# Writing y in natural channel order with 32-column matmul blocks, and loading w_in unpermuted

## The chip, the cores and the metric

The kernel runs on one core of a Trainium2 chip. The time is device microseconds of that core. Before the change the median of three runs is 618.56 us (617.26 to 618.66). The page and the trace come from one further, profiled execution, which took 619.2 us.

## What is computed

Two stages, in fp32 accuracy. First a gated linear attention over 4 batches, 8 heads, 768 tokens and head dimension 48, in which a 48x48 state decays by alpha and takes up the outer product of k and v. Then a feed-forward layer over the 3072 tokens, 384 channels (8 heads x 48) to 2048 and back, with a rational function between.

```python
for t in range(S):                                   # attention, per batch and head
    state = alpha[t][:, None] * state + outer(k[t], v[t])
    y[t] = q[t] @ state
x = y in token order, head by head                   # 3072 x 384
h = x @ w_in                                         # 384 -> 2048
P = a[0] + a[1]*h + a[2]*h**2 + a[3]*h**3
Q = 1 + abs(b[0])*abs(h) + abs(b[1])*h**2
out = (P / (Q + 1e-6)) @ w_out                       # 2048 -> 384
```

## The kernel before, in words

**Attention.** Tokens go in chunks of C = 128, two chunks to a segment (12 segments, `m`). A *piece* `i` is one chunk and four of the eight heads: chunk `g = i // 2`, head group `gq = i % 2`; 48 pieces in all. Within a piece heads are addressed by `a` (0 or 1) and `j` (0 or 1): head `2*gq + a + 4*j`. The group `j` sits on partitions 64j to 64j+47, since a head takes DP = 64 partitions of which D = 48 are used and GAP = 16 are not. alpha, k and q come to this channel-on-partition form in two ways: the first two segments are loaded by token (`load_nat`, L359) and transposed by TensorE (`turn_nat`, L367), the others are loaded in 32-row blocks (`load_akq`, L334) and transposed by VectorE (L383 to L389). v is loaded by token (`load_v`, L379) into a buffer with 64 columns a head, the last 16 zero.

Each piece runs these steps: `sc_mm` (L450) the scores, `sc_evac` on ScalarE (ACT) and `sc_mask` on GpSimd (POOL), `decay` (L473, POOL) which scales the state into `st_d`, and then `attn_mm` on TensorE (PE). `attn_mm` has three groups of matmuls: the state products (L486, not in the first chunk of a batch) and the value products (L493) add up y in PSUM bank 3, and the state update (L501, not in the last chunk of a batch) goes to a score bank. Each group is four products per piece, one for each (a, j); the stationary operand has 64 columns, so j = 0 writes partitions 0 to 63 and j = 1 writes 64 to 127. `kv_add` on VectorE (DVE) folds the update into the state. Scores are in banks 4 and 5; of the first EARLY = 4 pieces the odd ones are in banks 6 and 7, which are later the accumulators of the MLP output.

**From y to x.** y has four column slots of 128 tokens, one for each head pair, and in each the 16 partitions behind every group of 48 are zero. `x_hi` (L526, ACT) and `x_lo` (L531, DVE) copy the 512 columns of the bank into a high and a low part. `x_gap` (L541) then moves the rows of the fourth slot into the gaps of the first three by six transfers a segment (two j, three slots), so that three slots of 128 full partitions remain for the MLP. The channels are thereby permuted, and `load_w` (L221, L224) loads each unit of w_in in four transfers with the same permutation.

**MLP.** The hidden dimension goes in 8 units of 256. Per segment and unit (96 in all), `mlp_in` (L563) makes 18 matmuls of 256 columns (three partial products of high and low parts), fourteen elementwise steps on ACT, POOL and DVE (L570 to L613) make the rational function, and `mlp_out_hi` and `mlp_out_lo` (L624, L634) add the output in banks 6 and 7. The weights arrive as 64-bit words and are turned into a high and a low part on ACT, DVE and POOL (L237 to L268), once, in the first part of the run. At the end a guard over alpha (L660, L664) decides whether a general path is needed.

**Order.** Every step is registered with its engine, an assumed cost and the steps it comes after (`add`). The order in which all steps are issued is a written list, `ORDER`, a packed permutation of the step numbers, computed beforehand from those costs. Each engine and the transfer queue of SP (SyncE) run their share of this list in order. All loads and transfers of the fast path are issued by SP.

Of the kernel before, what the change touches and what calls it, by code (L numbers as in the profile page):

```python
# [12 lines left out]
F32 = mybir.dt.float32  # L13
F32R = mybir.dt.float32r
# [8 lines left out]
class Plan:  # L23
# [35 lines left out]
    'n3}92XwXMhM14qI2h_(^B<<mhdIyoUz)7`-qUZn~!d{B1Nn1FfPN`3zbs<ptE~EpaZ$n{74|gCJ6oCxz9&$r;T^v3@',
    '44oZ5LLP{v%fTZk3V9*6z6a$YAEeZA^#iB?adayE1*$><eOkrSpCO^Xq|U0;`U%9>_aUu*4ChsMs0bnYf+_*gbR}SX',  # L60
    '3KvyOoklyX42kq*m0pMHw-BcHQ3pt;Gw9s94op#rbsk+8GU^Ce5|ZdlI+@m(ROi*DAi2(`TS5w55Ay5MP*4}pnYCac',
    '9S-WlcPOlj=x6X18bDF)@j1ML7f?+9fc^9aitC1OfU@Wk`X?CBP*%5slDZm{(^++O$fo0Ad7WK<gNnKaG}IMzTs)^L',
    '>6%bkH_}tpFSw!lL1+CNYC#iSMK{(-u#0Z4tLiW;1C1duzJ#tihi<BK>IB#Xs_9(1g>I%x>FPQ@me#MKhHj|?ETe1c',
    '?z$-$9I9*SR=Tzhhr@Jh-9vZNaj=cPs)p-kkPt`eE9#nxh@*5{-5h%A>DuCT)lT=)Gjs_4f!;b1_R%+0dmV~>^<NmF',
    'TR=ZOQ-{aVdbS>;5$ouV@DKXyx_YbztfvR)aeAe04fXYSt+0V!r6*{@Hqb$@)*bagy;gV9ZDE$attRSwsvXSHbM<aL',
    'N#9a;)I7aMPu5Xzz8<6_V=la_*66`{fqtUa>&!Sr@73*Lp`N0%;UYa%FV_2YR-C5S=?%IE<iPWKiS7wmaHGDUd%-51',
    '6PM|Wx;NZc*>SU8s{6ne{ZLI)ePN&8s+a2r>asqlSLki}kbbEisfRi#9?*|;BrJ}P)nWZu@6hS-Aa#PB`iMS6+jS;<',
    'qL1pQDgz$VSM(+QOdZ$HbTN#IyYvZN0-vi>`l^nG8S%7!p`zn8{X-YUlR6n**U9mxzM)HFY<#M3>gW25E`z`HE&WQJ',
    ')hVzf{?UhNx{874bUEw{<?#r`!rS^Nb%DU#(Yf)i?h4_|3mx8cgWvk4j$r=jQus=PiHY}gf2e?Y@V<Vn%i;idt={Or',
    'x)HwBZ`1=l5b9zilM>%)H1+VUN`;~3y&eR$QJFA9=7Sy#bx@mkDzT}LL%^7%CNE|-4KSi%(*#rFNBv1R#waGT`K&+t',  # L70
    's3wc~=F{RA9nE~xUv)){Zp3`o)?_s?OjC3wrb&a|Br%;ZmdS29V{((sd{D7X3eyoks<<YOd9UJ`l%^pTHJ?;A(*;wR',
    'A1bGbZ@&9xm=05$VkU=4V?L_{rnpIK5}K0cs|qnQR63In6PfDf7=2U6DZR;HzNlO#qxq*wm>TB0%56%UOeR0pG-XUF',
    'lgIp21u(BEf@MuUQwV>nawfm2ZGNeirhqAL>X<*Of+=La_=={WDQqfZCDY1O!oRAP>4im1Yg5_OHGQy(X>014s-`!#',
    'F$J-=sc(8>d(+M|Fnvr{>|hEbP(#z#bjOaSkujvGlWA;bs{W=2b~e?_3F=}7m~J@MG%+WMsH<sanwnFD)Xg+E&9Q~)',
    'XS$mf_`~-w1C6Gh=BpoMdYLLX*o;M{A!ZEL!l5RhaptEVW~$;JUkz*Ea5LYG#tEi6jxY<%NE~k_n~`Rs8G+l(6tl>T',
    '!%1e8X^D%?XtTsj#AT)?jxkfsax)1Rn(bzq>5EIvc${v8c9<Dvg_(es9L+RyF*2<*o=%uqW<IVmyUc7e$E-G^aIRTn',
    'cAK4M9-cI7%^tG=Z<$kOo!M*7nBh3jw8GP7z1e5N(K&P0>^J941UgN#R0lj@TH^)N4iB0QCL)EWjpmTKXd=;Vv&EdD',
    'O=hc!NteuF^Tup8cg$sT#2htk@SeG1j+wjWzBz8Lng`~Wk3!eXL-WW)qqg|iTsP6_iD{2F%y0kH+%!??ua7|xJTq_2',
    '0DNx#nfK;}d1pSEm*#`{Y+jjx_|NylkLI-*guwlAA;zaKW->0r$UF=c55})%DMn%BZ)Pa2K;rKv7DeSBM)MYo&W6Ky',
    'w)$z9WAJ7?ONrU?Ir?RO8{zYmg#Q@FLogcuHJ$@b#&IYnhvVd&h2v5zUW8dWHpS-fJO$(M5{$s{C@v@Eh`b%+adr-)',  # L80
    'NSuOqU`|dzDLEJK#Q2<wLue}Q!UUX+OLJ;YNC|llCZaSP!fAOQmf=v!!Ra^!?Zrf#o6~bBm*w4<hcj?SUWs{m8)o8Z',
    'SdKIE8O+BOxh|LI>39lfVI{_(9-qeiT!Cj`0ZvROu|5~%IarxzVtX#cbJTLYKt;GPSK*7a6&rF<uF4I#7&qc-ycnx<',
# [24 lines left out]
    '0#{Fcm5xfegf5b+uR`2dis;Biagkjj_f)idCdM^X-z2IFbKiwsG?&<or=cpkn?OG#hRfn&I_oA<Ea#lKaTMEm*Fnvo',
# [27 lines left out]
GB = 3  # L135
# [844 lines left out]
```

## Time and profile before

| | |
|---|---|
| median of 3 runs | 618.56 us (617.26 to 618.66) |
| profiled execution | 619.2 us, span of the trace 617.3 us |
| busy: PE / DVE / ACT / POOL | 553.9 / 507.6 / 477.8 / 387.4 us |
| mean granted TensorE clock | 0.957 |
| L486 state products, L493 value products, L501 state update | 320, 384, 320 matmuls; 28.1, 32.2, 16.5 us |
| L526 `x_hi`, L531 `x_lo` | 24 each; 14.1 and 16.4 us |
| L541 `x_gap` | 72 transfers of 32 KB, median 2.0 us from issue to landing |
| L221, L224 w_in | 16 transfers of 288 KB and 16 of 96 KB, median 5.7 and 5.6 us |

A row of a group gives the source line, engine, operation, operands, shape and count, then busy time and the mean length of one in ns, then the idle time just before and what ended it. Busy time of overlapping matmuls is counted once, so busy time over count can be less than the mean length. PEld is the loading of the stationary operand. The ends of matmuls are modelled in the trace; their starts are recorded. A row of the timeline gives start, length to the end of the last, and the count of instructions that were merged.

### The profile page before, as it was taken

The page shows a single profiled execution, that of the slowest core. Times are in us where ns is not written, and L with a number is a line of the kernel's source. Part 1 is how long each engine was busy: PE and PEld are TensorE (multiplying, and loading weights), DVE is VectorE, ACT ScalarE, POOL GpSimd, SP SyncE. Part 2 cuts the span into 40 slices and gives each one's busy share as a digit, 9 for nine tenths or more (in the row PEclk, how much of TensorE's full clock was granted, in tenths as well). Part 3 has the DMA queues.
Part 4 walks back from the last instruction along what each step waited for, and adds up shares of the span by engine and source line. Part 5 has one row for each costly group of instructions (what it writes and reads, how often), then busy time and mean ns, then how long its engine had stood idle before and what let it go on. Part 6 is the DMA issues. An engine that isn't in the chain of part 4 may idle for free.

```text
span 617.3 us, 12165 instructions
## 1 busy us (share of the span) xinstructions
PE 553.9 (90%) x4338; PEld 515.4 (83%) x4338; DVE 507.6 (82%) x782; ACT 477.8 (77%) x803; POOL 387.4 (63%) x419
## 2 busy tenths in 40 slices
PE   3866857899699999999999999999899999999993
PEld 2656746788599989999999999899899999999983
DVE  3588898999989988889888987989789787777872
ACT  3467666777668788987889898999878787888971
POOL 4645234676687686867768676667648667655561
PEclk9977887899899999999999999999899999999997
DMA  9999495413452441344324343434321000000000
GB/s 154 227 189 251 77 188 103 54 19 50 61 101 47 93 53 50 54 82 65 64 57 77 57 85 67 90 65 91 55 44 36 14 27 14 14 22 6 27 2 30
DMA packets 182658, 44.14 MB, mean 71 GB/s; under 512 B 170944, under 2 KB 174016, under 8 KB 182592
## 3 DMA queue, kind: packets, MB, share of 16 engines
q1 hardware_dynamic: 182592, 43.30, 38.0%
q8 instruction: 36, 0.59, 0.4%
q14 instruction: 30, 0.25, 0.1%
HBM read 36.18 MB, written 4.72 MB: 66 GB/s over the span
## 4 chain that ended last, share of the span: by engine, by line
PE 49%; DVE 21%; ACT 11%; DMA 9%; SPq 4%; issue 3%; POOL 1%; ACTq 0%; DVEq 0%; POOLq 0%
PE ps L563 20%; PE ps L624 14%; PE ps L634 7%; DMA wi_words<-in_moe_w_in_dram 5%; DVE t L597 4%; DVE ps L600 3%; DVE t L606 3%; PE ps L450 3%; ACT t L573 2%; PE ps L486 2%; DVE t L587 2%; SPq L334 2%; DVE t L583 2%; PE ps L493 2%; DMA tv<-in_v_dram 2%
## 5 line engine op out<-in xcount | busy, mean ns | idle before, releaser
L563 PE MATMUL ps<-x,wi 128*128 128x256 f32 x1728 | 235.9, 289 | 23.5 <-DVE t L606 14.7
L563 PEld LDWEIGHTS ps<-x,wi 128*128 128x128 f32 x1728 | 223.2, 194 | 33.9 <-DVE t L606 20.1
L579 POOL TENSOR_TENSOR qm<-qm,ah 128x512 f32<-128x512 f32 x96 | 128.4, 1338 | 101.8 <-ACT qm L576 100.8
L624 PE MATMUL ps<-wo,gh 128*128 128x384 f32 x768 | 159.8, 348 | 6.3 <-ACT gh L609 3.5
L613 POOL TENSOR_TENSOR gl<-t,gh 128x512 fp32r<-128x512 f32 x88 | 116.5, 1326 | 51.5 <-issue 28.8
L624 PEld LDWEIGHTS ps<-wo,gh 128*128 128x128 f32 x768 | 134.7, 192 | 12.2 <-ACT gh L609 6.7
L583 DVE TENSOR_TENSOR t<-t,ps 128x512 f32<-128x512 f32 x96 | 65.4, 681 | 36.9 <-ACT t L573 29.5
L597 DVE SCALAR_TENSOR_TENSOR t<-t,coef,ps 128x512 f32<-128x512 f32 x96 | 71.3, 742 | 24.4 <-ACT ps L593 24.0
L634 PE MATMUL ps<-wo,gl 128*128 128x384 f32 x384 | 85.9, 346 | 4.1 <-DVE gl L613 4.1
L573 ACT ACTIVATE t<-ps,coef 128x512 f32<-128x512 f32 x96 | 74.3, 774 | 12.0 <-PE ps L563 5.3
L576 ACT ACTIVATE qm<-ah,bab 128x512 f32<-128x512 f32 x96 | 77.8, 810 | 6.8 <-DVE ps L600 5.5
L590 ACT ACTIVATE ps<-qm,one_eps 128x512 f32<-128x512 f32 x96 | 66.0, 688 | 20.0 <-DVE t L587 15.1
L609 ACT ACTIVATE gh<-t 128x512 fp32r<-128x512 f32 x96 | 60.0, 625 | 19.9 <-DVE t L606 18.1
L570 ACT ACTIVATE ah<-ps 128x512 f32<-128x512 f32 x96 | 56.9, 593 | 23.7 <-PE ps L563 23.0
L634 PEld LDWEIGHTS ps<-wo,gl 128*128 128x128 f32 x384 | 68.9, 192 | 5.9 <-DVE gl L613 4.4
L587 DVE SCALAR_TENSOR_TENSOR t<-t,coef,ps 128x512 f32<-128x512 f32 x96 | 71.6, 746 | 2.6
L606 DVE SCALAR_TENSOR_TENSOR t<-ps,t 128x512 f32<-128x512 f32 x96 | 66.0, 687 | 2.2
L600 DVE SCALAR_TENSOR_TENSOR ps<-qm,ps 128x512 f32<-128x512 f32 x96 | 66.0, 688 | 0.0
L593 ACT ACTIVATE ps<-ps 128x512 f32<-128x512 f32 x96 | 56.1, 584 | 1.3
L450 PE MATMUL ps<-tq,tk 48*128 48x192 f32 (+1 forms) x384 | 46.8, 366 | 9.5 <-POOL tq L425 9.5
L459 ACT ACTIVATE sc<-ps 128x768 f32<-128x768 f32 (+1 forms) x48 | 36.9, 769 | 12.7 <-PE ps L450 8.4
L450 PEld LDWEIGHTS ps<-tq,tk 48*128 48x128 f32 x384 | 32.3, 203 | 16.4 <-POOL tq L425 10.8
(93 smaller groups left out, 609.5 us busy)
## 6 DMA issues: line engine op xcount, KB each, us to landing
wo_words<-in_moe_w_out_dram SPq DMA_DIRECT2D x8, 768.0 KB, 8.1
wi_words<-in_moe_w_in_dram SPq DMA_DIRECT2D x16, 288.0 KB, 5.7
tv<-in_v_dram SPq DMA_DIRECT2D x24, 192.0 KB, 3.1
wr<-in_alpha_dram SPq DMA_DIRECT2D x18, 256.0 KB, 2.9
out_dram<-parts SPq DMA_DIRECT2D x24, 192.0 KB, 2.0
raw_a<-in_alpha_dram SPq DMA_DIRECT2D x80, 32.0 KB, 2.1
raw_q<-in_q_dram SPq DMA_DIRECT2D x80, 32.0 KB, 2.1
raw_k<-in_k_dram SPq DMA_DIRECT2D x80, 32.0 KB, 2.1
```

Source lines behind the costliest of these rows:

```text
L450: nc.tensor.matmul(bank(home(i) + j)[:, SW * a : SW * a + w], tk[n % NQ][r, c, :], tq[n % NQ][r, c, 0:w], start=True, stop=True,)
L563: nc.tensor.matmul(h_of(u)[:, ff * SEG : (ff + 1) * SEG], split_w["i", j][:, kt * FU + ff, w, :], x[:, kt, xp, :], start=(kt == 0 and n == ...
L573: nc.scalar.activation(buf(s, "t1", u), h_of(u), AF.Identity, bias=a2, scale=a3)
L576: nc.scalar.activation(buf(s, "qm", u), buf(s, "ah", u), AF.Identity, bias=b0, scale=b1)
L579: nc.gpsimd.tensor_tensor(buf(s, "qm", u), buf(s, "qm", u), buf(s, "ah", u), op=ALU.mult)
L587: nc.vector.scalar_tensor_tensor(t, t, a1, h_of(u), op0=ALU.add, op1=ALU.mult)
L597: nc.vector.scalar_tensor_tensor(t, t, a0, h_of(u), op0=ALU.add, op1=ALU.mult)
L600: nc.vector.scalar_tensor_tensor(h_of(u), buf(s, "qm", u), 1.0 + 1e-6, h_of(u), op0=ALU.add, op1=ALU.mult)
L606: nc.vector.scalar_tensor_tensor(t, h_of(u), 2.0, t, op0=ALU.subtract, op1=ALU.mult)
L613: (nc.vector if GL_DVE[0] <= u < GL_DVE[1] and s is fast_bufs else nc.gpsimd).tensor_tensor(buf(s, "gl", u).rearrange("p a b -> p (a b)"), ...
L624: nc.tensor.matmul(o_of(tt), buf(s, "gh", u)[:, ff, tt * P : (tt + 1) * P], split_w["o", j][:, ff, w, :], start=(j == j0 and ff == 0 and w ...
L634: nc.tensor.matmul(o_of(tt), buf(s, "gl", u)[:, ff, tt * P : (tt + 1) * P], split_w["o", j][:, ff, 0, :], start=False, stop=(j == j1 and f ...
```

## The change

y is written in the order of the 384 channels themselves: three column slots of 128 tokens, all partitions used, no gaps. A head begins at channel 48h, which is a multiple of 32 for even a and 16 behind one for odd a. So the window of 64 columns that holds a head and 16 zero columns (ahead of the head for a = 1, behind it for a = 0) always begins at a multiple of 32. It is written as two matmuls of 32 stationary columns, each to one quarter of the partitions, and the zeros add nothing to the neighbouring head that shares the quarter (`into_y`). The state update is cut into blocks of 32 columns too. The buffers of v and of the decayed state get 16 zero columns ahead of the first head. `x_hi` and `x_lo` copy 384 columns instead of 512, `x_gap` and its 72 transfers are gone, the MLP follows `x_lo` directly, and each unit of w_in is one transfer. EARLY is 8 instead of 4. `ORDER` is a new list; the costs that the list was made with are 0.47 and 0.55 for `x_hi` and `x_lo` and one transfer's cost for a unit of w_in, and those of `attn_mm` are as before. The general path is changed alike and left out here.

```diff
--- before.py
+++ after.py
@@ -51,73 +51,73 @@
 ORDER = [
...
 ]
@@ -126,7 +126,7 @@
 DMA = 0.49
 W_ACT = {}
 PHASES = (0, 6)
-EARLY = 4
+EARLY = 8
 NQ = 3
 LO_DVE = (0, 4)
 GL_DVE = (0, 8)
@@ -195,7 +195,6 @@
-
     NI = FU * P
     w_in32 = w_in.bitcast(U32)
     w_out32 = w_out.bitcast(U32)
@@ -214,17 +213,7 @@
         eng = nc.scalar if j in W_ACT else nc.sync
         if kind == "i":
             t = weights.tile([P, KT, 2 * NI], U32, tag=f"wi{j}", name=f"wi{j}_words")
-            cols = w_in32[:, 2 * j * NI : 2 * (j + 1) * NI]
-            for jj in range(2):
-                h0 = jj * NPAIR * D
-                h3 = h0 + KT * D
-                eng.dma_start(
-                    t[DP * jj : DP * jj + D], cols[h0:h3].rearrange("(a p) n -> p a n", p=D)
-                )
-                eng.dma_start(
-                    t[DP * jj + D : DP * (jj + 1)],
-                    cols[h3 : h3 + D].rearrange("(a p) n -> p a n", p=GAP),
-                )
+            eng.dma_start(t, w_in32[:, 2 * j * NI : 2 * (j + 1) * NI].rearrange("(a p) n -> p a n", p=P))
         else:
             t = weights.tile([P, FU, 2 * DM], U32, tag=f"wo{j}", name=f"wo{j}_words")
             eng.dma_start(t, w_out32[j * NI : (j + 1) * NI, :].rearrange("(a p) n -> p a n", p=P))
@@ -285,11 +274,12 @@
     tk = ring("tk", NQ, [P, NC4, C])
     tq = ring("tq", NQ, [P, NC4, C + DP])
     ones1 = work.tile([P, NC4 * C1], F32, name="ones1")
-    tv = ring("tv", 3, [P, H, DP])
+
+    tv = ring("tv", 3, [P, GAP + H * DP])
     tot = ring("tot", NQ, [P, NC4, 2])
     halves = work.tile([P, 2], F32, name="halves")
     st_s = ring("st_s", 2, [P, 2, D])
-    st_d = ring("st_d", 2, [P, 2, 2, DP])
+    st_d = ring("st_d", 2, [P, GAP + NPAIR * DP])
     scs = ring("sc", NSC, [P, 2, 2, C + DP])
     def set_raw(s, nm):
@@ -314,7 +304,11 @@
             )
     def set_v(s):
-        nc.gpsimd.memset(tv[s][:, :, D:DP], 0.0)
+        nc.gpsimd.memset(tv[s][:, 0 : H * DP].rearrange("p (h w) -> p h w", w=DP)[:, :, 0:GAP], 0.0)
+        nc.gpsimd.memset(tv[s][:, H * DP :], 0.0)
+
+    def heads_of(t):
+        return t[:, GAP:].rearrange("p (h w) -> p h w", w=DP)[:, :, 0:D]
     def set_st():
         nc.gpsimd.memset(halves, 0.0)
@@ -376,7 +370,7 @@
     def load_v(g):
         b, t0 = divmod(g * C, S)
-        nc.sync.dma_start(tv[g % 3][:, :, 0:D], v[b, :, t0 : t0 + C, :].rearrange("h t e -> t h e"))
+        nc.sync.dma_start(heads_of(tv[g % 3]), v[b, :, t0 : t0 + C, :].rearrange("h t e -> t h e"))
     def turn_a(n):
         o = ta[n % 2][:, 1:].rearrange("p (c t) -> p c t", t=C1)[:, :, 0:C]
@@ -471,37 +465,49 @@
         g, gq, m, cc, first, last, n = piece(i)
         f = tot[n % NQ][:, cc::2, :]
         nc.gpsimd.tensor_tensor(
-            st_d[gq][:, :, :, 0:D], st_s[gq].unsqueeze(2).to_broadcast([P, 2, 2, D]),
+            heads_of(st_d[gq]).rearrange("p (a j) e -> p a j e", j=2),
+            st_s[gq].unsqueeze(2).to_broadcast([P, 2, 2, D]),
             f.unsqueeze(3).to_broadcast([P, 2, 2, D]), op=ALU.mult,
         )
+
+
+
     def attn_mm(i):
         g, gq, m, cc, first, last, n = piece(i)
         sc, vt = scs[i % NSC], tv[g % 3]
         y = bank(3)
+        begun = set() if gq == 0 else set(range(4))
+
+        def into_y(lhs, at, rhs, a, j, stop):
+            c0 = D * (2 * gq + a + NPAIR * j) - GAP * a
+            for x in range(2):
+                kt, r = divmod(c0 + 32 * x, P)
+                w0 = GAP + DP * at - GAP * a + 32 * x
+                nc.tensor.matmul(
+                    y[r : r + 32, kt * C : (kt + 1) * C], lhs[:, w0 : w0 + 32], rhs,
+                    start=r // 32 not in begun, stop=stop, skip_group_check=True,
+                )
+                begun.add(r // 32)
+
         if not first:
             for a in range(2):
-                p = 2 * gq + a
                 for j in range(2):
-                    nc.tensor.matmul(
-                        y[DP * j : DP * (j + 1), p * C : (p + 1) * C], st_d[gq][:, a, j, :],
-                        tq[n % NQ][:, 2 * a + cc, 0:C], start=(p == 0), stop=False, skip_group_check=True,
-                    )
+                    into_y(st_d[gq], 2 * a + j, tq[n % NQ][:, 2 * a + cc, 0:C], a, j, False)
         for a in range(2):
-            p = 2 * gq + a
             for j in range(2):
-                nc.tensor.matmul(
-                    y[DP * j : DP * (j + 1), p * C : (p + 1) * C], vt[:, p + NPAIR * j, :],
-                    sc[:, j, a, 0:C], start=(first and p == 0), stop=(p == NPAIR - 1), skip_group_check=True,
-                )
+                into_y(vt, 2 * gq + a + NPAIR * j, sc[:, j, a, 0:C], a, j, gq == 1)
         if not last:
             kv = bank(home(i) + i % 2)[:, KV : KV + 2 * D]
             for a in range(2):
                 for j in range(2):
-                    nc.tensor.matmul(
-                        kv[DP * j : DP * (j + 1), a * D : (a + 1) * D], sc[:, j, a, C:],
-                        vt[:, 2 * gq + a + NPAIR * j, 0:D], start=True, stop=True,
-                    )
+                    h = 2 * gq + a + NPAIR * j
+                    for x in range(2):
+                        r = DP * j + 32 * x
+                        nc.tensor.matmul(
+                            kv[r : r + 32, a * D : (a + 1) * D], sc[:, j, a, C + 32 * x : C + 32 * (x + 1)],
+                            vt[:, GAP + DP * h : GAP + DP * h + D], start=True, stop=True,
+                        )
     def kv_add(i):
         g, gq, m, cc, first, last, n = piece(i)
@@ -518,27 +524,20 @@
 ORDER = [
...
 ]
@@ -729,21 +728,14 @@
...
@@ -796,7 +788,7 @@
     keys = [(kind, j) for j in range(NU) for kind in "io"]
     for n, key in enumerate(keys):
-        add(("w", key), "ACT" if key[1] in W_ACT else "SP", 4 * DMA if key[0] == "i" else DMA, load_w, key, kb=2.4,
+        add(("w", key), "ACT" if key[1] in W_ACT else "SP", DMA, load_w, key, kb=2.1,
             at=W_ACT.get(key[1], 0.0))
         add(("abs", key), "ACT", 0.91, join_abs, (key, n), [("w", key)] + [("lo", x) for i, x in enumerate(keys[:n]) if wr_slot(i) == wr_slot(n)][-1:])
         add(("sign", key), "DVE", 0.55, join_sign, (key,), [("abs", key)], lock=True)
@@ -879,10 +871,8 @@
     last_user = {6: [i for i in range(EARLY) if home(i) == 6]}
     for g in range(NBLK * 2):
         m, cc = divmod(g, 2)
-        add(("xh", g), "ACT", 0.6, x_hi, (g,), [("am", 2 * g + 1), ("last", m - XB)])
-        add(("xl", g), "DVE", 0.7, x_lo, (g,), [("xh", g)])
-        if cc:
-            add(("xg", m), "SP", 6 * 0.63, x_gap, (m,), [("xl", g), ("xl", g - 1)], kb=0.6)
+        add(("xh", g), "ACT", 0.47, x_hi, (g,), [("am", 2 * g + 1), ("last", m - XB)])
+        add(("xl", g), "DVE", 0.55, x_lo, (g,), [("xh", g)])
     ends = {}
@@ -892,7 +882,7 @@
             early = [("cp", *key, 2 * key[0] + x) for key in nat_users[u % 3] for x in range(2)]
             early += [("tn", 1, nm, cc) for nm in "akq" for cc in range(2)]
             add(("in", u, ff), "PE", 1.08, mlp_in, (u, ff, xts[m % XB]),
-                [("xg", m), ("lo", ("i", j)), ("in", u, 0) if ff else ("in", u - 1, FU - 1), ("g", u - 3)]
+                [("xl", 2 * m), ("xl", 2 * m + 1), ("lo", ("i", j)), ("in", u, 0) if ff else ("in", u - 1, FU - 1), ("g", u - 3)]
                 + early, lat=0.13, due=T0 + PACE * u + 1.08 * (ff + 1))
         if j == NU - 1:
             add(("last", m), "PE", 0.0, lambda: None, (), [("in", u, 1)])
```

More of the change, by code (lines that the diff above doesn't have):

```diff
@@ L59 @@
[L59 to L70, printed above, removed]
@@ new lines @@
+    '7hh2_H5p&hTRMjOu!>5qUei0;k15m}I*7&874@D{t3%jbrBsLU1Eo;~)Jcr5j$libMg62xm_Yrak8~Ovsf6kiox#s^',
+    '6#q~Ml~o<b-;_vYQ(q{pnu5FO1d94gd+0n~!ka3mQu-gA#R~}fhDxVUUst5R(k+!<X?+p1tIOC=Wl-f*ke-TH(5T{y',
+    'bwJ%!k@Q{?ZPgvMkG_#tMn6`;`a1=w`zo@w`UkyN<yDAw`kC_jfePpf>Ygg7DyoO7kgB8}sa&eC`k=z}b5%rrRG~Ut',
+    '-&QZwQ&m|-(dY1+imIdOcj}F*ql&5@>WR96arGyaTgB5JqU%>Gy^f*d>+gz{R(VuRok4$933P<ctLm!Hs)S0Y>!~2f',
+    'q)V!d`mM^W>#G1H)>(7|C6HAo(TTK!Z2F5TrIPAoT0=fnS|!&FRb+^zv+EQ(wyvryq||YA4qZkCLqXk2<<tzRbRk_$',
+    'rPh%kjV`RKD+6hD5nV$S)#-Fq{ZiFb)$}h_OXboDpt>%uYwEa=TfbI~RSDf($A_P)n9ieH=n#kvC3Rk%PiKNZs+7Kp',
@@ L121 @@
+    '#}Dvb`~*MHcl8tfAV1Gf@@xEHKi^OGYyA{I#8376{5n6)&-Fw72EX4g@az3TztIo#2mB^K+%NK*{dB+BZ}Bty62H|i',
+    '^)r25zs(==%lu)#-Cyv_{SLpvU-UcuO25k=^sD@3f5fl$SNu`G+h6t9{T_eJU-LKoUVq$Q@+bUFf70Lbr~GYy+TZbK',
+    '{TYAPpY!+pd4JzO@DKeX|I|PB&-@er9}QKs$p',
 ]
@@ L531, in x_lo @@
         nc.vector.tensor_tensor(
-            xts[m % XB][:, :, 1, cs], bank(3).rearrange("p (k t) -> p k t", t=C),
+            xts[m % XB][:, :, 1, cs], bank(3, DM).rearrange("p (k t) -> p k t", t=C),
             xts[m % XB][:, :, 0, cs].bitcast(F32), op=ALU.subtract,
         )
-    def x_gap(m):
-        x = xts[m % XB].bitcast(F32).rearrange("p k w t -> p k (w t)")
-        for j in range(2):
-            for kt in range(KT):
-                r0 = DP * j + GAP * kt
-                nc.sync.dma_start(x[DP * j + D : DP * (j + 1), kt], x[r0 : r0 + GAP, KT])
     N = FU * SEG
@@ L731, in general @@
                 for tt in range(2):
-                    xn = gen.tile([P, KT, 2, DP], F32, name=f"gen_x{tt}")
+                    xn = gen.tile([P, H, D], F32, name=f"gen_x{tt}")
                     tok = bass.ds(r0 + tt * P, P)
-                    for jj in range(2):
-                        h0 = jj * NPAIR
-                        nc.sync.dma_start(
-                            xn[:, :, jj, 0:D], xd[h0 : h0 + KT, tok, :].rearrange("h t e -> t h e")
-                        )
-                        nc.sync.dma_start(
-                            xn[:, :, jj, D:DP],
-                            xd[h0 + KT, tok, :].rearrange("t (k e) -> t k e", e=GAP),
-                        )
+                    nc.sync.dma_start(xn, xd[:, tok, :].rearrange("h t e -> t h e"))
                     xp = bank(3, DM)
@@ L745, in general @@
                         nc.tensor.transpose(
-                            xp[:, kt * P : (kt + 1) * P], xn[:, kt].rearrange("p j e -> p (j e)"), ident
+                            xp[:, kt * P : (kt + 1) * P],
+                            xn.rearrange("p h e -> p (h e)")[:, kt * P : (kt + 1) * P], ident,
                         )
```

117 lines of the change are left out of this document (60 added, 57 removed).

## The prediction

> **What bounds the kernel now.** I read the table of stretches first, for the engine that is full in each stage, then the waits, then the timeline where the edits fall. Columns: stretch; its length; busy time and count of PE, PEld, DVE, ACT and POOL; granted clock; DMA share; GB/s.
>
> ```profile
> 0.00:20.00 20.00, 7.77 (x32) 5.44 (x32) 9.69 (x12) 6.77 (x15) 9.66 (x34) 1.00 1.12 159
> 20.00:40.00 20.00, 15.60 (x132) 12.29 (x128) 11.33 (x18) 11.43 (x23) 11.76 (x17) 0.97 1.08 246
> 40.00:60.00 20.00, 13.17 (x100) 11.71 (x100) 18.06 (x25) 14.35 (x20) 8.44 (x13) 0.67 0.90 193
> 80.00:100.00 20.00, 12.64 (x76) 11.13 (x77) 18.76 (x29) 11.03 (x17) 8.07 (x11) 0.76 0.83 158
> 100.00:150.00 50.00, 44.87 (x338) 41.33 (x338) 46.93 (x70) 38.68 (x61) 31.41 (x27) 0.96 0.35 55
> ...
> 200.00:550.00 350.00, 345.26 (x2880) 326.59 (x2879) 297.37 (x474) 298.46 (x515) 242.24 (x248) 1.00 0.31 56
> ```
>
> Three stages can be seen. Up to 40 us the DMA engines are full (shares 1.12 and 1.08) and no engine is. From 40 to about 150 us VectorE (DVE) is the full one, 18.06 of 20, 18.76 of 20, 46.93 of 50. From 200 to 550 us TensorE (PE) is busy 345.26 of 350 us: there a microsecond of matmul is a microsecond of the run, and time saved on ACT, DVE or in the queues is worth at most the 4.7 us that PE stands idle.
>
> **The change part by part: matmuls.** This decides the sign. The products for y and for the key-value state each become two, with 32 stationary columns instead of 64. So the question is whether narrower blocks run side by side. The timeline around 210 us has one piece in the middle of PE work (start, length, line, form, count), and under it the same value products in windows that end 0.11 us later each time:
>
> ```profile
> 209.71 0.66 PE L486 MATMUL ps<-tq,st_d 128*64 128x128 f32 x8
> 210.19 0.61 PE L493 MATMUL ps<-sc,tv 128*64 128x128 f32 x8
> 210.63 0.39 PE L501 MATMUL ps<-tv,sc 128*64 128x48 f32 x8
> 210.95 0.39 PE L563 MATMUL ps<-x,wi 128*128 128x256 f32 x1
> ```
> ```profile
> 210.19 0.28 PE L493 MATMUL ps<-sc,tv 128*64 128x128 f32 x2
> 210.19 0.39 PE L493 MATMUL ps<-sc,tv 128*64 128x128 f32 x4
> 210.19 0.50 PE L493 MATMUL ps<-sc,tv 128*64 128x128 f32 x6
> ```
> ```profile
> 32.30 0.33 PE L367 MATMUL ps<-ident,qm 128*128 128x128 f32 x1
> 32.30 0.44 PE L367 MATMUL ps<-ident,qm 128*128 128x128 f32 x2
> 32.30 0.55 PE L367 MATMUL ps<-ident,qm 128*128 128x128 f32 x3
> 32.30 0.66 PE L367 MATMUL ps<-ident,qm 128*128 128x128 f32 x4
> ```
>
> A piece has four value products in the code and eight matmuls in the trace, so an fp32 product is two matmuls. They are counted in twos: two more every 0.11 us. The control is the transpose, 128 fp32 columns streamed through the whole array: one more every 0.11 us. So one such matmul takes 0.11 us of its block either way, and two blocks of 64 columns (j = 0 and j = 1) run at once: 8 matmuls are 4 steps of 0.11 = 0.44 us, which is the distance from 210.19 to 210.63.
>
> After the change a full piece has 16 value matmuls on four blocks of 32 columns. Four at a time that is again 4 steps, 0.44 us: no cost. Two at a time it is 8 steps, 0.88 us: 0.44 more, and the same for the state products. Both ends in total, from the counts after 200 us:
>
> ```profile
> 200.00:617.30 417.30, 20.23 (x264) 15.28 (x264) 0.99 0.27 50
> ...
> 200.00:617.30 417.30, 19.07 (x232) 12.07 (x232) 0.99 0.27 50
> ...
> 200.00:617.30 417.30, 10.47 (x216) 9.96 (x216) 0.99 0.27 50
> ```
>
> These are L493, L486 and L501. Two at a time adds (264 + 232)/2 x 0.11 = 27.3 us where PE is the bound. I take zero: the row shows blocks of one array running independently, and the second matmul of a product does not hold up the first one of its neighbour although it stands ahead of it in the program.
>
> [...]
>
> The state update (L501) is shorter, 48 columns:
>
> ```profile
> 210.63 0.21 PE L501 MATMUL ps<-tv,sc 128*64 128x48 f32 x2
> 210.63 0.39 PE L501 MATMUL ps<-tv,sc 128*64 128x48 f32 x8
> ```
>
> Three steps lie between 0.21 and 0.39, 0.06 each. Streaming alone would be 48/128 of 0.11, 0.04. If 16 matmuls go four at a time, 4 steps of 0.04 to 0.06 give 0.16 to 0.24 us against 0.24 now; if they only go at today's rate of one per 0.03 us, 0.48. Over 216/8 = 27 pieces that is -2 to +6.5 us. I take zero, four steps of 0.06 as in the row.
>
> **Row transfers, evacuation, loads.** The first MLP unit shows what the copies of x cost:
>
> ```profile
> 37.49 0.68 DVE L531 TENSOR_TENSOR x<-ps,x 128x512 fp32r<-128x512 f32 x1
> 38.20 6.52 SPq L541 DMA_DIRECT2D x<-x  x6
> 46.06 5.88 PE L563 MATMUL ps<-x,wi 128*128 128x256 f32 x36 [1.07 <-DMA x<-x]
> ```
> ```profile
> PE ps L563 <- DMA x<-x: 1.1, 1, 1.1
> ```
>
> x is ready at 38.17, the six issues hold SP until 44.72, and PE starts at 46.06. The wait row says that this is the only time in the first 200 us that PE waited for one. The unit can start up to 46.06 - 38.17 = 7.9 us earlier. SP's six issues go too, so the loads behind them move up by as much.
>
> ```profile
> L221 SPq DMA_DIRECT2D wi_words<-in_moe_w_in_dram x16: 312/424/1323, 0.8 to 88.9; - x16
> L224 SPq DMA_DIRECT2D wi_words<-in_moe_w_in_dram x16: 420/436/1521, 1.3 to 89.4; - x16
> ```
>
> ```profile
> 79.87 1.64 PE L634 MATMUL ps<-wo,gl 128*128 128x384 f32 x4 [4.06 <-DVE gl L613]
> ```
>
> Of 32 issues 8 remain: 24 x 0.43 = 10.3 us of SP, in a stage where SP feeds saturated DMA engines; bytes are equal, so only part turns into earlier landing. The written order of the steps moves as well: decoded, it puts the weights ahead of the raw loads on SP's queue, and pieces 5 and 7 now use banks 6 and 7 too, so that the first MLP output must wait behind piece 7 on PE's queue. All this ends in the stage where DVE is full. It has 19.0 us of idle before 40 us (40 - 9.69 - 11.33) and only 6.3 in the three later stretches shown (90 - 18.06 - 18.76 - 46.93), so DVE can follow an earlier start only in part. I take 5 us saved. The ends are 9 saved (the 7.9 and a little of SP's) and 4 lost (piece 7 comes late and the first outputs stand behind it; the price is about one of today's waits of an output product, 4.1 in the row for L634).
>
> ```profile
> L526 ACT ACTIVATE x<-ps 128x512 fp32r<-128x512 f32 x24 | 14.1, 588 | 3.3 <-PE ps L493 3.0 <-DMA raw_a<-in_alpha_dram 0.2
> L531 DVE TENSOR_TENSOR x<-ps,x 128x512 fp32r<-128x512 f32 x24 | 16.4, 684 | 2.5 <-ACT x L526 2.4
> L646 ACT ACTIVATE parts<-ps 128x384 f32<-128x384 f32 x24 | 10.8, 485 | 5.4 <-PE ps L634 5.4
> L644 DVE TENSOR_TENSOR parts<-parts,ps 128x384 f32<-128x384 f32 x4 | 2.1, 549 | 0.3 <-PE ps L634 0.3
> ```
>
> x_hi and x_lo shrink from 512 to 384 columns. By the 384-column rows ACT saves 24 x (588 - 485) = 2.5 us and DVE 24 x (684 - 549) = 3.2 us. I cost this at nothing, because PE covers it after 200 us; if PE gets slack it is worth up to 3.2. The wider v buffer costs one small memset each, under POOL's start.
>
> **The sum.** The profiled execution took 619.2 us (span 617.3 and 1.9 around it), 0.6 above the median 618.56. 619.2 - 5 + 0 + 0 = 614.2, less 0.6 to the median: 613.6, say 614. Its own range is 605 (9 saved, 2 from the state update, some slack used) to 617.
>
> **Rivals.** *Two blocks at a time* (the slower side). One mechanism: the second matmul of each product occupies the queue, so adding blocks adds steps. For it: nothing in the trace shows more than two at once, and four blocks would read four streams from the same 128 partitions at once, which no row shows. Against it: the lockstep pairs. It adds 27.3 after 200 us, 6.5 for the state update (216/2 x 0.06), and before 200 us perhaps half of the remaining counts (120 + 88 value and state, (208/2) x 0.11 = 11.4, halved 5.7), hidden half by PE's idle there:
>
> ```profile
> 0.00:200.00 200.00, 11.93 (x120) 8.89 (x120) 0.90 0.63 117
> 0.00:200.00 200.00, 9.05 (x88) 5.80 (x88) 0.90 0.63 117
> ```
>
> 613.6 + 27.3 + 6.5 + 5.7 = 653; range 641 to 665. It decides once a fourth block does not start beside the first.
>
> *Issue limit between the two.* Four blocks run, but matmuls cannot be handed out faster than about one per 0.03 us, or only three blocks overlap: +6.5 for the state update up to a third of 27.3 + 5.7 plus that (17.5), a little more with stalls where two neighbouring products share a block. 613.6 + 6.5 to 613.6 + 25: 620 to 639, middle 629.
>
> *Hidden anyway.* Matmuls cost nothing, and the earlier start is swallowed by the full DVE between 40 and 150 us: 617 to 620, the present time.
>
> **Numbers.** 0.3% is 1.9 us, about what a measurement of this kernel can tell from no change. Forecast (605 to 617): 0.48. Hidden anyway: 0.14. Issue limit: 0.18. Two at a time: 0.20. So faster 0.48, same 0.14, slower 0.38. The range goes from 605 to 652: it takes in the first three cases and nearly half of the last, and leaves out a little below 605.
>
> **What would show it.** Right: the value products of a full piece, now 16, still take 0.44 us from the first to the next group, and are counted in fours per 0.11 us; no transfer x<-x; the first MLP matmul near 40 us; from 200 us on PE as full as before with the same total. Wrong: 16 value matmuls in 0.88 us (two at a time), a PE total 30 us and more higher in the rows after 200 us, or a first MLP output that comes later than its present 61.74 us:
>
> ```profile
> 61.74 2.93 PE L624 MATMUL ps<-wo,gh 128*128 128x384 f32 x8
> ```

## The result, and the profile after

The changed kernel takes 602.36 us (median of 4 runs, 600.71 to 604.26), against 618.61 us (617.26 to 621.52) of the kernel before in the runs beside it. The ratio is 0.9732, with a 95% interval of 0.9685 to 0.9779. That is a gain of 16.2 us where 4.6 were forecast: the direction was right, and the time lies below the range. The profiled execution took 600.71 us, with a span of 599.0.

The table of stretches of the changed kernel, in the columns and stretches of the first fence of the prediction:

```profile
0.00:20.00 20.00, 10.10 (x40) 6.87 (x40) 8.59 (x10) 7.71 (x17) 15.29 (x42) 1.00 1.24 168
20.00:40.00 20.00, 16.24 (x248) 12.74 (x251) 15.06 (x24) 12.45 (x24) 12.27 (x15) 1.00 1.03 328
40.00:60.00 20.00, 15.29 (x238) 13.12 (x234) 18.10 (x29) 16.70 (x23) 12.08 (x20) 0.83 0.90 299
80.00:100.00 20.00, 12.85 (x81) 12.31 (x80) 19.93 (x29) 14.20 (x22) 8.99 (x6) 0.83 0.33 41
100.00:150.00 50.00, 43.36 (x403) 39.35 (x406) 45.55 (x70) 38.64 (x62) 32.43 (x31) 0.93 0.25 32
200.00:550.00 350.00, 349.42 (x3622) 332.46 (x3621) 302.95 (x484) 307.00 (x530) 250.36 (x252) 1.00 0.28 50
```

The last two columns of the second and third row show what the forecast did not have. The DMA engines are as full as before (shares 1.03 and 0.90, before 1.08 and 0.90), but in that time they move 328 and 299 GB/s where they moved 246 and 193. Part of that is what the new list sends first: the same code in the old list (e1 below) moves 307 and 200. DVE has 15.06 us of work between 20 and 40 us where it had 11.33. In the last row PE is busy 349.42 of 350 us (before 345.26).

The same from the page's list of DMA queues (packets, which are the single pieces that an engine moves; MB; share of 16 engines), the kernel before first and the changed one second:

```profile
q1 hardware_dynamic: 182592, 43.30, 38.0%
```
```profile
q1 hardware_dynamic: 179904, 40.94, 34.9%
```

38.0% of 617.3 us is 234.6 us of all 16 engines, 34.9% of 599.0 is 209.1: 25.5 us less (11%) for 5% fewer bytes, those of the row transfers.

The timeline of the changed kernel at one piece after 200 us, and under it its state products in windows that end 0.11 us later each time:

```profile
203.13 0.64 PE L487 MATMUL ps<-tq,st_d 128*32 128x128 f32 x16
203.59 0.62 PE L487 MATMUL ps<-sc,tv 128*32 128x128 f32 x16
204.03 0.35 PE L507 MATMUL ps<-tv,sc 128*32 128x48 f32 x16
204.31 1.33 PE L562 MATMUL ps<-x,wi 128*128 128x256 f32 x9
```
```profile
203.13 0.32 PE L487 MATMUL ps<-tq,st_d 128*32 128x128 f32 x4
203.13 0.42 PE L487 MATMUL ps<-tq,st_d 128*32 128x128 f32 x8
203.13 0.54 PE L487 MATMUL ps<-tq,st_d 128*32 128x128 f32 x12
203.13 0.64 PE L487 MATMUL ps<-tq,st_d 128*32 128x128 f32 x16
```

Twice as many matmuls take the same time: 16 value matmuls lie between 203.59 and 204.03, 0.44 us, and they are counted in fours. The whole piece, from the first product to the next MLP matmul, takes 1.18 us (203.13 to 204.31), before 1.24 (209.71 to 210.95).

The start of the MLP in the changed kernel's timeline:

```profile
33.51 0.36 PE L562 MATMUL ps<-x,wi 128*128 128x256 f32 x1
34.44 2.27 PE L562 MATMUL ps<-x,wi 128*128 128x256 f32 x17 [0.56 <-DVE x L537]
...
59.81 1.55 PE L623 MATMUL ps<-wo,gh 128*128 128x384 f32 x8
```

The first MLP matmul is at 33.51 us (46.06 before), the first output product at 59.81 (61.74 before).

### The profile page after: what moved, and what is told of

Read it like the earlier page. It is cut to its first block, busy times and chain, and to the rows that moved or that the text cites. A ratio compares the mean times of both kernels' runs of the same rounds, so it can differ in the third digit from the quotient of the medians.

```text
span 599.0 us, 14096 instructions
## 1 busy us (share of the span) xinstructions
PE 540.2 (90%) x5362; PEld 503.4 (84%) x5362; DVE 503.8 (84%) x782; ACT 475.5 (79%) x803; POOL 400.3 (67%) x422
## 3 DMA queue, kind: packets, MB, share of 16 engines
q1 hardware_dynamic: 179904, 40.94, 34.9%
## 5 line engine op out<-in xcount | busy, mean ns | idle before, releaser
L562 PE MATMUL ps<-x,wi 128*128 128x256 f32 x1728 | 232.7, 287 | 16.2 <-ACT wi L250 7.4
L562 PEld LDWEIGHTS ps<-x,wi 128*128 128x128 f32 x1728 | 220.9, 192 | 26.4 <-ACT wi L250 7.8
L623 PE MATMUL ps<-wo,gh 128*128 128x384 f32 x768 | 157.6, 344 | 16.2 <-DVE wo L257 6.7
L623 PEld LDWEIGHTS ps<-wo,gh 128*128 128x128 f32 x768 | 132.3, 190 | 21.3 <-DVE wo L257 6.9
L633 PE MATMUL ps<-wo,gl 128*128 128x384 f32 x384 | 84.4, 342 | 0.3 <-POOL gl L612 0.3
L608 ACT ACTIVATE gh<-t 128x512 fp32r<-128x512 f32 x96 | 60.1, 626 | 18.1 <-DVE t L605 16.0
L457 POOL TENSOR_SCALAR_AFFINE_SELECT sc<-sc 128x512 f32<-128x512 f32 x48 | 31.9, 666 | 20.3 <-ACT sc L453 19.8
```

Of the source, the lines that this page charges most:

```text
L562: nc.tensor.matmul(h_of(u)[:, ff * SEG : (ff + 1) * SEG], split_w["i", j][:, kt * FU + ff, w, :], x[:, kt, xp, :], start=(kt == 0 and n == ...
L623: nc.tensor.matmul(o_of(tt), buf(s, "gh", u)[:, ff, tt * P : (tt + 1) * P], split_w["o", j][:, ff, w, :], start=(j == j0 and ff == 0 and w ...
L633: nc.tensor.matmul(o_of(tt), buf(s, "gl", u)[:, ff, tt * P : (tt + 1) * P], split_w["o", j][:, ff, 0, :], start=False, stop=(j == j1 and f ...
```

## The experiments

Twelve kernels ran, in three groups. Each group has its own runs of the kernel before beside it (617.85, 617.91 and 617.88 us), so kernels of different groups are compared by ratio. Differences in us are those of the medians; where the ratio says something else, that is given too.

| kernel | median us | ratio | 95% interval |
|---|---|---|---|
| the change | 602.36 | 0.9732 | 0.9685 to 0.9779 |
| e1 the change, old written order | 604.41 | 0.9803 | 0.9728 to 0.9878 |
| e2 before, new written order | 636.41 | 1.0304 | 1.0243 to 1.0365 |
| e3 before, no row transfers | 612.25 | 0.9926 | 0.9894 to 0.9958 |
| e4 the change, products sorted by block | 605.75 | 0.9803 | 0.9740 to 0.9867 |
| e5 = e3, copies of 384 columns | 612.08 | 0.9909 | 0.9875 to 0.9943 |
| e6 = e5, one load per unit of w_in | 608.07 | 0.9839 | 0.9800 to 0.9877 |
| e7 the change, all of y in one block | 698.88 | (one run) | |
| e8 = e1, four loads per unit | 613.13 | 0.9912 | 0.9883 to 0.9942 |
| e9 = e1, three loads of 128 partitions | 606.20 | 0.9820 | 0.9784 to 0.9855 |
| e10 the change, four loads per unit | 620.76 | 1.0058 | 1.0031 to 1.0086 |
| e11 before, one load per unit | 609.69 | 0.9868 | 0.9838 to 0.9898 |
| e12 the change, one load later | 604.40 | 0.9792 | 0.9767 to 0.9818 |

My first theory, A, was that the new written order gives the gain: the edits had been costed at 5 us, and the order was the one part that I had hardly costed. The rival was that the edits give it under any order.

**e1: the change with the old written order.** The new code, run in the list of before without the row transfers, and with EARLY as before.

```diff
 ORDER = [
...
 ]
-EARLY = 8
+EARLY = 4
```

> The changed kernel, but its steps issued in the written order of before (less the twelve row transfers) and EARLY = 4. Theory A (most of the 16 us comes from the new written order: fewer switches of TensorE between attention and MLP and fewer stalls after 200 us; the edits themselves give about the 5 us of the forecast): 611 to 616 us. Rival B (the edits give it: no row transfers, narrower evacuation, four blocks at once; the order only follows): 600 to 605 us.

Measured 604.41 us, 13.4 below the kernel before. Theory A fell: the edits give most of the gain without the new list. The interval of e1 overlaps that of the change, so what the list adds (about 2 us by the medians) is not resolved.

**e2: the kernel before with the new written order.** Its row transfers stand behind the second `x_lo` of each segment.

```diff
 ORDER = [
...
 ]
-EARLY = 4
+EARLY = 8
```

> The kernel before, with 64-column products, four w_in transfers a unit and the row transfers, but issued in the written order of after (each segment's six row transfers put behind its second x_lo) and EARLY = 8. Theory A (order): 606 to 613 us, as the transfers cost some of the early lead and about 2.5 us of matmuls are missing. Rival B (edits): 616 us or more, as the new order gains nothing without them.

Measured 636.41 us, 18.6 slower. The new list on the old code is a loss. e2's group of the MLP's input products, and two of its stretches with all engines, show where:

```profile
L560 PE MATMUL ps<-x,wi 128*128 128x256 f32 x1728 | 236.3, 290 | 29.5 <-DMA x<-x 9.9
```
```profile
20.00:40.00 20.00, 12.27 (x125) 9.71 (x124) 9.26 (x17) 9.14 (x18) 9.43 (x12) 0.90 1.11 205
40.00:60.00 20.00, 7.87 (x53) 6.47 (x51) 8.41 (x12) 6.32 (x10) 7.40 (x6) 0.59 0.93 245
```

PE waits 9.9 us for the row transfers, and between 40 and 60 us DVE, the full engine of that stage before (18.06 of 20), is busy 8.41.

**e3: only the row transfers gone.** The fourth slot does not reach the MLP.

```diff
-        if cc:
-            add(("xg", m), "SP", 6 * 0.63, x_gap, (m,), [("xl", g), ("xl", g - 1)], kb=0.6)
...
-                [("xg", m), ("lo", ("i", j)), ("in", u, 0) if ff else ("in", u - 1, FU - 1), ("g", u - 3)]
+                [("xl", 2 * m), ("xl", 2 * m + 1), ("lo", ("i", j)), ("in", u, 0) if ff else ("in", u - 1, FU - 1), ("g", u - 3)]
```

> The kernel before in its own order, without the row transfers: the MLP follows x_lo directly, so the fourth slot of each head group's channels is left out of the product. Theory A: 613 to 618 us, only the first MLP unit starts up to 7.9 us earlier and the full VectorE eats most of it. Rival B: 603 to 608 us, as the transfers and the waits of SP behind them were the cost.

Measured 612.25 us, 5.6 faster (2.6 to 6.5 by the interval). The row transfers alone were worth about what the forecast gave to rows, loads and order together. So some 8 us of e1's 13.4 had to come from the load, the copies or the blocks.

**e4: the products of a piece sorted by block.** All products that write one block of 32 partitions stand together, the next block behind them. The heart of the edit; the state update is sorted alike:

```diff
...
+            for r, kt, lhs, w0, rhs, stop in sorted(calls, key=lambda c: c[0]):
                 nc.tensor.matmul(
                     y[r : r + 32, kt * C : (kt + 1) * C], lhs[:, w0 : w0 + 32], rhs,
...
```

> The changed kernel with the same 16 state, 16 value and 16 update matmuls of a piece, sorted by the block of 32 columns that they write, so that neighbours in the program share a block. If TensorE looks far ahead for a free block (deep lookahead), the groups still take 0.44 us and the run stays at 602 us. If it only lets the next product or two pass (short lookahead), a group takes between 0.9 and 1.8 us, 1 to 3 us more a piece, and the run is 30 to 95 us longer.

Measured 605.75 us, 3.4 above the change; the intervals overlap, so this is not resolved. One piece in e4's timeline, and its state products in windows that end later each time:

```profile
205.25 0.66 PE L491 MATMUL ps<-tq,st_d 128*32 128x128 f32 x16
205.71 0.66 PE L491 MATMUL ps<-sc,tv 128*32 128x128 f32 x16
206.14 0.41 PE L515 MATMUL ps<-tv,sc 128*32 128x48 f32 x16
206.48 1.33 PE L570 MATMUL ps<-x,wi 128*128 128x256 f32 x9
```
```profile
205.25 0.34 PE L491 MATMUL ps<-tq,st_d 128*32 128x128 f32 x4
205.25 0.45 PE L491 MATMUL ps<-tq,st_d 128*32 128x128 f32 x8
205.25 0.55 PE L491 MATMUL ps<-tq,st_d 128*32 128x128 f32 x12
```

Still fours, and 0.43 us between the value products and the update. As written, the last block's first matmul has twelve others ahead of it. The trace does not name the block of a matmul; but if the four matmuls of one block go one per 0.11 us (e7 below), four steps suffice only when every block, the last too, starts in the first step.

**e5: e3 with copies of 384 columns.** This asks for the price of `x_hi` and `x_lo` alone.

```diff
-        nc.scalar.activation(o, bank(3).rearrange("p (k t) -> p k t", t=C), AF.Copy)
+        nc.scalar.activation(o, bank(3, DM).rearrange("p (k t) -> p k t", t=C), AF.Copy)
```

> The kernel before in its own order without row transfers (e3), and x_hi and x_lo copying 384 columns, the three slots that the MLP reads (the fourth slot's channels stay left out). The order theory has fallen, so the remaining 8 us between e3 (612.3) and e1 (604.4) lie in the narrower copies, the single w_in transfer or the 32-column blocks. Theory C (copies are worth little, since TensorE covers them after 200 us): 611 to 613 us. Rival D (they shorten the stage in which VectorE is full): 607 to 609 us.

Measured 612.08 us, as e3. The copies did get shorter, by the groups of e5:

```profile
L527 DVE TENSOR_TENSOR x<-ps,x 128x384 fp32r<-128x384 f32 x24 | 13.2, 552 | 1.9 <-ACT x L522 1.7
L522 ACT ACTIVATE x<-ps 128x384 fp32r<-128x384 f32 x24 | 11.5, 480 | 3.3 <-PE ps L489 3.2
```

DVE gave back 3.2 us (16.4 to 13.2) and ACT 2.6, and the end did not move by anything that these runs resolve (the intervals of e3 and e5 overlap).

**e6: e5 with one load per unit of w_in.** Channels meet other rows of w_in than they should; bytes and work are the same.

```diff
-            for jj in range(2):
...
+            eng.dma_start(t, w_in32[:, 2 * j * NI : 2 * (j + 1) * NI].rearrange("(a p) n -> p a n", p=P))
```

> As e5, and each unit of w_in loaded by one transfer in its natural row order, so that channels of x meet other rows of w_in than they should. Theory C (the weights land sooner and the full VectorE starts its long list sooner): 4 us below e5, 607 to 609 us. Rival D: no change from e5.

Measured 608.07 us, 4.0 below e5 by the medians; the two intervals just touch. The profiled span is 603.3 us, that of e1 603.1. By the medians e6 stands 3.7 above e1, by the ratios 2.2, and the intervals overlap: what is left between the two (the blocks) is not resolved.

**e7: all of y in one block.** Every product of y writes the first 32 partitions, so the sums are not y; the count and size of the matmuls are those of the change.

```diff
-                kt, r = divmod(c0 + 32 * x, P)
+                kt, r = (c0 + 32 * x) // P, 0
```

> The changed kernel with all state and value products of a piece written to the first quarter of the partitions, one block of 32 columns, so that the other three quarters of y are not computed. If blocks run at once because they are different blocks: the 16 matmuls of a group go one after the other, 16 x 0.11 = 1.7 us instead of 0.44, about 2.6 us more a full piece, some 90 to 110 us more in all. If a matmul of 32 columns is merely four times shorter: 602 us as before.

Measured 698.88 us, 96.5 above the change. A piece of e7 in its timeline, and the count of its first products:

```profile
240.22 1.93 PE L487 MATMUL ps<-tq,st_d 128*32 128x128 f32 x16
241.99 1.80 PE L487 MATMUL ps<-sc,tv 128*32 128x128 f32 x15
```
```profile
240.22 0.30 PE L487 MATMUL ps<-tq,st_d 128*32 128x128 f32 x1
240.22 0.41 PE L487 MATMUL ps<-tq,st_d 128*32 128x128 f32 x2
240.22 0.51 PE L487 MATMUL ps<-tq,st_d 128*32 128x128 f32 x3
```

Sixteen matmuls take 1.77 us (240.22 to 241.99), 0.11 each, one after another. So the four at a time of the change hang on their writing different blocks.

**e8: e1 with four loads per unit.** Natural rows, but cut by partitions as in the kernel before: 48, 16, 48 and 16.

```diff
-            eng.dma_start(t, w_in32[:, 2 * j * NI : 2 * (j + 1) * NI].rearrange("(a p) n -> p a n", p=P))
+            rows = w_in32[:, 2 * j * NI : 2 * (j + 1) * NI].rearrange("(a p) n -> p a n", p=P)
+            for p0, p1 in ((0, D), (D, DP), (DP, DP + D), (DP + D, P)):
+                eng.dma_start(t[p0:p1], rows[p0:p1])
```

> The changed kernel in the written order of before (e1), with each unit of w_in loaded by four transfers of 48, 16, 48 and 16 partitions, the sizes of before. Theory C: 4 us above e1 (604.4), 607 to 610 us. Rival D: as e1, 604 to 605 us.

Measured 613.13 us: the cut alone gives back 8.7 of e1's 13.4 us (6.7 of 12.2 by the ratios), more than expected. The first 60 us of e1, then of e8 (stretch, length, DVE busy and count, granted clock, DMA share, GB/s):

```profile
0.00:20.00 20.00, 11.69 (x12) 1.00 1.24 169
20.00:40.00 20.00, 13.96 (x23) 0.87 1.01 307
40.00:60.00 20.00, 17.80 (x26) 0.67 0.70 200
```
```profile
0.00:20.00 20.00, 9.67 (x12) 1.00 1.24 151
20.00:40.00 20.00, 10.06 (x16) 0.93 1.09 211
40.00:60.00 20.00, 17.82 (x24) 0.67 1.12 204
```

The DMA engines are full in both up to 40 us, but in e8 they move 211 GB/s instead of 307 between 20 and 40, and stay full until 60 us where e1's have room (1.12 against 0.70). DVE loses 5.9 us of work in the first 40 us (25.65 against 19.73). Where the queue is late shows in the timeline of SP, at the first w_in load and at the fourth group of block loads of alpha, 18.1 us later in e8. e1 stands first; the view of e8 ends at 62 us and so counts one issue of that group:

```profile
0.80 0.45 SPq L212 DMA_DIRECT2D wi_words<-in_moe_w_in_dram  x1
...
41.35 7.46 SPq L324 DMA_DIRECT2D raw_a<-in_alpha_dram  x4
```
```profile
0.81 1.82 SPq L214 DMA_DIRECT2D wi_words<-in_moe_w_in_dram  x4
...
59.45 3.21 SPq L326 DMA_DIRECT2D raw_a<-in_alpha_dram  x1
```

e8 had two differences left from e1: more issues on SP, and loads that each reach few partitions. The third group separates them. Theory E holds that the loads themselves are slow when they reach few partitions; theory F that SP's issues cost it.

**e9: e1 with three loads per unit, each to all 128 partitions.** More issues, packets of the same 2 KB.

```diff
-            eng.dma_start(t, w_in32[:, 2 * j * NI : 2 * (j + 1) * NI].rearrange("(a p) n -> p a n", p=P))
+            rows = w_in32[:, 2 * j * NI : 2 * (j + 1) * NI].rearrange("(a p) n -> p a n", p=P)
+            for kt in range(KT):
+                eng.dma_start(t[:, kt], rows[:, kt])
```

> e1 (changed kernel, written order of before) with each unit of w_in loaded by three transfers of 128 partitions and 256 KB. Theory E (a transfer to 48 or 16 partitions keeps the DMA engines busy nearly twice as long per 2 KB packet, 187 ns in e8 against 98 ns in e1, and the first 60 us are bound by these engines): as e1, 603 to 606 us. Rival F (the number of issues on SP, 0.43 us each, is the cost): two thirds of the way from e1 to e8, 609 to 611 us.

Measured 606.20 us, ratio 0.9820: its interval lies apart from that of e8 and overlaps that of e1. F falls as the main cause. That the issues cost nothing is not shown: e9 is 1.8 us above e1 by the medians (1 by the ratios), and in its profiled execution DVE has 22.9 us of work before 40 us, between the 25.7 of e1 and the 19.7 of e8. The DMA queue's rows of e1, e8 and e9 in this order:

```profile
q1 hardware_dynamic: 179904, 40.94, 35.0%
```
```profile
q1 hardware_dynamic: 180288, 40.94, 38.4%
```
```profile
q1 hardware_dynamic: 180160, 40.94, 34.6%
```

For the same bytes e1 needs 35.0% of 603.1 = 211 us of all 16 engines, e9 34.6% of 605.7 = 210, e8 38.4% of 611.4 = 235. In the trace's packet records the 3072 packets of w_in (2 KB each) take 98 ns on average in e1, 97 in e9, 95 in the change, but 187 in e8, 181 in e10 and about 165 in the kernel before. 3072 x (187 - 98) ns over 16 engines is 17 of the 24 us between e8 and e1; the rest lies in other packets and was not taken apart. What e8's loads share and e9's do not is the partitions reached; whether their packets are also spread otherwise over the 16 engines, no run separates.

**e10: the change with four loads per unit.** The edit of e8, under the new written order.

> The changed kernel in its own new order, with each unit of w_in loaded by four transfers of 48, 16, 48 and 16 partitions. The new order puts all of w_in ahead of the raw loads on SP, so theory E expects it to lose more than the 8.7 us between e1 and e8: 611 to 622 us, with first MLP outputs later than 61.7 us. If the order did not depend on the loads: 611 us or less.

Measured 620.76 us, 18.4 above the change and 2.9 above the kernel before; the first output product comes at 73.9 us, late as expected. The first large group of block loads of alpha on SP's timeline, in the change and in e10:

```profile
50.80 6.53 SPq L328 DMA_DIRECT2D raw_a<-in_alpha_dram  x8
```
```profile
67.38 9.06 SPq L330 DMA_DIRECT2D raw_a<-in_alpha_dram  x8
```

Under the new order most of the weights stand ahead of these loads on SP's queue, so slow weight loads delay them by 16.6 us, close to the loss. With slow loads the new list loses (e8 613.13, e10 620.76); with fast loads it does not (e1 604.41, the change 602.36).

**e11: the kernel before with only the load changed.** Row transfers stay; channels meet other rows of w_in. The edit is that of e6.

> The kernel before, row transfers and all, with each unit of w_in loaded by one transfer in natural row order, so that channels of x meet other rows of w_in than they should. Theory E: 4 to 8 us below before, 610 to 614 us. If the single load only pays once the row transfers are gone: 617 to 619 us.

Measured 609.69 us, 8.2 faster (6.3 to 10.0 by the interval). This is the part that the forecast missed, by itself. The page of e11 has each unit as one load, with its median time to landing:

```profile
wi_words<-in_moe_w_in_dram SPq DMA_DIRECT2D x8, 768.0 KB, 5.7
```

768 KB to all partitions land in the 5.7 us that 288 KB to 48 partitions took in the kernel before.

**e12: the change, with the first unit of w_in behind the first two loads of alpha.** Only the list differs.

```diff
 ORDER = [
...
 ]
```

> The changed kernel with the first unit of w_in put behind the two first alpha loads on SP's queue, so that TensorE's first transpose starts about 2 us earlier and the first weights land about 2 us later. If the attention chain sets the start: 600 to 601 us. If the weights' chain on VectorE does, or both: 602 to 604 us.

Measured 604.40 us: no gain, though the first transpose does start earlier (4.52 us, in the change 7.04). None of the twelve measured faster than the changed kernel.

## Why the prediction was right or wrong

**The gain has two terms.** Row transfers 5.6 us (e3) and load 8.2 (e11) make 13.8; e1, which has both and the blocks and copies, shows 13.4 (7.5 to 16.8 by the interval). They add up as far as these runs can tell. The load's price is known less well than one run says: 8.2 on the kernel before, 8.7 between e1 and e8 (6.7 by the ratios), 4.0 between e5 and e6. The new list brings about 2 more under fast loads, which is not resolved.

**The step that failed** is the load's: "bytes are equal, so only part turns into earlier landing". Bytes are equal, but the time that the engines need for them is not. I had costed 24 issues on SP at 0.43 us each, and discounted that because the DMA engines behind SP were full (shares 1.12 and 1.08 up to 40 us). By e9 the issues are the smaller part at most (1.8 of 8.7 us by the medians); what counts is how long the full DMA engines take for a packet, and that fell by two fifths (165 to 95 ns). The best end of the term, 9 us, was the 7.9 of the rows and a little of SP's, so it held next to nothing for the load, which by itself measured 8.2 (e11). The trace of the kernel before held a hint that I did not use: in it 288 KB of w_in took 5.7 us to land and 96 KB took 5.6, so a load a third as large took as long. It is a hint only, since two loads that wait in the same queue could land alike for that reason; the packet times are the plainer sign.

Packet by packet it is 187 ns for loads of 48 and 16 partitions (e8) against 97 for loads of 128 partitions in three parts (e9). The runs here show that difference; what makes a packet of the narrow loads take longer, no run shows.

**Where the time came back.** The prediction held that DVE, full between 40 and 150 us (18.06 of 20, 18.76 of 20 and 46.93 of 50 us in its stretches), could follow an earlier start only in part. It had counted DVE's 19.0 us of idle before 40 us and put them to little use; but DVE's work there hangs on the loads, and it moved: 21.0 us of DVE work before 40 us in the kernel before (9.69 + 11.33), 25.7 in e1, 23.7 in the change. The lead can be followed by the units of the MLP (a unit is one segment and one of the 8 parts of the hidden dimension). The last four output products of the 16th unit, in the kernel before, e1 and e8:

```profile
182.80 0.87 PE L634 MATMUL ps<-wo,gl 128*128 128x384 f32 x4
```
```profile
172.76 0.87 PE L629 MATMUL ps<-wo,gl 128*128 128x384 f32 x4
```
```profile
180.78 0.87 PE L631 MATMUL ps<-wo,gl 128*128 128x384 f32 x4
```

The last of each four starts at 183.3, 173.3 and 181.3 us. From there to unit 96 e1 and e8 take almost the same, 422.3 and 423.3 us; e9 lies between at 177.1, with 422.0 behind it. So nearly all of the load's effect, 8.0 us, is a lead made before unit 16 and kept.

The new list spends it otherwise. In the change unit 16 comes at 179.7, and unit 96 at 591.9, 412.2 us later. All kernels have issued the same 13 pieces of attention by unit 16, so the two parts can be compared over all of them. From unit 16 to unit 96 those with the new list and no row transfers (the change, e4, e10, e12) take 412.2 to 415.1 us, those with the old list and no row transfers (e1, e3, e5, e6, e8, e9) 422.0 to 424.1. So there the new list gains some 10 us, with slow loads too. Before unit 16 it loses: 6.4 us with fast loads (179.7 in the change, 173.3 in e1) and 18.2 with slow ones (199.5 in e10, 181.3 in e8). With the row transfers (e2) the gain is missing, 425.7 us against 426.5 in the kernel before, and unit 16 comes at 203.2. The stretch after 200 us on PE, kernel before, e1, and the change:

```profile
200.00:617.30 417.30, 401.40 (x3243) 0.99 0.27 50
```
```profile
200.00:603.10 403.10, 387.34 (x3841) 0.99 0.25 46
```
```profile
200.00:599.00 399.00, 388.29 (x3877) 1.00 0.25 46
```

PE's idle there is 15.9 us in the kernel before, 15.8 in e1 and 10.7 in the change. The new list ends the first stage with a smaller lead than e1 and leaves PE 5 us less idle afterwards. Which of its moves does that stays open, and so does whether the change is faster than e1 at all: these are single profiled executions, and by the medians only about 2 us are left.

**Matmuls at zero: right.** Sixteen take 0.44 us and are counted in fours, the sign that the prediction had named. PE's busy time after 200 us, which two at a time would have raised by some 30 us, fell from 401.40 to 388.29; "the same total" it is not, and that difference was not taken apart. Two at a time (653 us) and the issue limit (629) are both wrong: e8, which has the blocks, stands at 0.9912 beside e5's 0.9909, which has not. The rival's mechanism, a product's second matmul that holds up the next block, no run shows: in the change four start within 0.02 us. e7 shows the reason that the prediction assumed, blocks that run independently (0.44 us for sixteen on four blocks, 1.77 on one), and what the opposite would cost (96.5 us).

**State update at zero: right, a little on the good side.** 16 in 0.28 us (204.03 to 204.31), before 8 in 0.32.

**Copies at nothing: right** as far as e3 and e5 resolve it, and with the prediction's cover: PE is full after 200 us (345.26 of 350 us before, 349.42 in the change).

**Rows: within their bound.** 5.6 us, where up to 7.9 were allowed; the term of 5 was meant for rows, loads and order together, so that it lies close to 5.6 is chance. The page of the changed kernel has no transfer from x to x, and the first MLP matmul comes at 33.51 us, earlier than the 40 that rows alone had let expect.

**Piece 7 and the first outputs.** Against the kernel before the feared delay did not come: the first output is at 59.81 us. Against the same code in the old list it did, in part: e1 has its first output at 57.32 us, and its lead of 6.4 us at unit 16 is more than the 4 us that the prediction had set for this; whether piece 7 is what costs it is not shown. What it did not have is the gain of the new list after unit 16. With slow loads the order costs 18 us (e2, e10).

**Hidden anyway** (617 to 620) is wrong: 0.9732 leaves 1 out by far.

## What to carry to other kernels

Where the DMA engines are the full resource (here with shares of 1.24 and 1.01 in the first 40 us of e1), cost a transfer by the time of its packets, not by its bytes alone or by the number of its issues: compare packet times with those of transfers of the same packet size to other partition counts (98 ns in e1, 187 in e8, for the same 2 KB). Landing times are a weaker sign: the same 768 KB land in 6.2 us in e1 and in 8.9 in the change, at packets of 98 and 95 ns. A lead made in the first stage can come through whole, even if the engine of the next stage looks full (e1 against e8: 8.0 us at unit 16 and 9.0 at unit 96, with DVE busy 17.8 of 20 us between 40 and 60 us in both). A written order belongs to the durations that it was made with: try a new order and the edits apart, since the order alone may lose what both together gain.

## What the runs showed of the hardware

In e4 matmuls of different blocks did not keep the order of the program: each block's four stand together as written, and the sixteen still take 0.46 us (205.25 to 205.71). Started strictly in that order, with the 0.11 us of e7 between two of one block, they would need 13 steps, about 1.4 us. In the records the first four starts lie 0.013 us apart, in the change, where fewer stand between one block and the next, 0.007. In e7 the matmuls, all of one block, do go one after another (0.11 us each, +96.5 us). The recorded starts show this; the ends are modelled and show nothing of it.

The changed kernel's matmuls of 48 columns start faster than the prediction's rate of one per 0.03 us: sixteen in 0.28 us (204.03 to 204.31), 0.0175 each, with the change to the next stationary operand in it.
